# A three-part network on one core: one expert's slot search moves in line, its transposes later, and second products may run ahead

## The chip, the cores and the metric

The kernel runs on one core of a Trainium2 chip. The metric is the device time of one execution in microseconds (us); lower is better. Five engines work side by side, each through its own queue in order: PE (matrix products, transposes), DVE and ACT (elementwise work), POOL (here mostly a queue that starts DMAs with computed addresses or with addition) and SP (starts plain DMAs). "PEld" in the profile is the loading of a matmul's stationary operand.

## The reference, cut to what matters

```python
x = attention(r, k, v, w, u)               # 3072 tokens x 384, linear attention with decay
h = x @ w_in                               # dense part, 2048 hidden
x = (h * sigmoid(1.702 * h)) @ w_out
logits = x @ w_gate                        # 3072 x 8 experts
order = argsort(-logits.flatten())         # all (token, expert) pairs, best first
for idx in order:                          # greedy, each token once, each expert cap = 384 tokens
    tok, e = idx // E, idx % E
    if assigned[tok] >= 0 or counts[e] >= cap: continue
    assigned[tok] = e; counts[e] += 1
for e in range(8):                         # experts: 384 -> 1024 -> 384
    mask = assigned == e
    out[mask] = relu(x[mask] @ w1[e]) @ w2[e]
```

## The kernel before, in words

The first 580 us are the attention and the dense part, which the change does not touch. What follows is the part with the eight experts. They are handled in the order in which they fill up, and are called expert 0 to expert 7 here after that order. Two strands of work run side by side.

The first strand is the routing (`Router.route`, L304). For each expert in turn it

- searches (`search`, L382) for the threshold at which the next expert is full. A search has five rounds, each a comparison on DVE (L279), 24 small matmuls (L424), a small matmul (L429) and a maximum on DVE (L431), and each round needs the one before;
- writes the number of the expert found (`ei`, L323). From then on its weights can be loaded;
- ranks the tokens taken (L344 to L351), while the first steps for the next search (`best`, L236) are interleaved;
- marks the tokens that are left (`left`, L365) and goes on to the next search (its first instruction is L415).

Ranks must be turned into a list of 384 token numbers, `idx`. That is `slots` (L455): comparisons with 128 numbers on DVE (two of L476), 24 small matmuls (L487) and three small DVE steps, the last of which (L496) writes `idx`. For the first three experts (i <= 2, L358) `slots` runs in line, that is before the route goes on to `left` and the next search. For later ones `gather` (L1463) calls it, as a chain of its own that shares the engines with the next search.

`gather` then starts three indirect DMAs on POOL (L1476), which fetch 128 token rows each from `x2d` in device memory into the tile `cvb`. For each of the three, `land` (L1487) lets PE make three transposes (L1492), ACT a rounded copy (`xh`, L1501) and DVE the remainder (`xl`, L1503). When all three are through, the expert's products can begin (`o["ffn"]`, L1542).

The weights of an expert come as eight plain loads of 384 KB (L1415, SP). ACT makes the rounded half (L1434), and the remainder comes either from ACT (L1451) and a DMA with addition started on POOL (L1457), or from one DVE instruction (L1442). POOL also starts the scatter of the results (L1535).

The second strand is the loop of products (L1582), which consists of 64 steps, 8 to an expert. Step s issues a first product G1(s) (nine matmuls, L1086, reading `xh`, `xl` and the first weights) and then the second product G2(s-2) (nine matmuls, L1114). ACT and DVE turn the result of G1 into the input of G2 between them.

The order of all queues is written out while the program is built. A planner (`Issue`, L66) keeps a planned clock and planned busy times for each engine and for the DMA engines ("D"); each chain of work is a generator that yields until its planned time has come. `sc.until(cond)` (L117) advances the planned clock until the condition holds, issues whatever chain is due, and meanwhile issues small filler matmuls (`spin`, L687, line L690 in the profile). PE executes its queue in the order so written. If the planned time at which a transpose was placed is earlier than the real landing of its rows, PE stands still at that place, and all behind it with it.

The planned landing of gather a is `xt[a]`, the planned DMA time plus 1.4 (L1479). `land` waits for it, and for `LATE` = 4.0 more if the loop of products is still more than three steps ahead of the expert (`at[0] < NF3 * i - 3`, L1488). The loop waits for expert i at its first step (L1586), and only then issues G1 and the second product of two steps before.

Of the kernel before, what the change touches and what calls it, by code (L numbers as in the profile page):

```python
# [162 lines left out]
class Router:  # L163
# [140 lines left out]
    def route(self, out, i, found, taken):  # L304


        nc, NJ, E, L, t = self.nc, self.NJ, self.E, self.L, self.t
# [47 lines left out]
            n = next(fill, "end")  # L355
            yield from self.vec(0.22 if n == "end" else 0.47)
        out["rs"] = rs
        if i <= 2:  # L358
            yield from self.slots(out)
        taken()  # L360
        if i == E - 1:
# [139 lines left out]
def kernel(ctx, tc, r, k, v, w, rk, u, us, w_in, w_out, w_gate, w1, w2, out):  # L501
    nc = tc.nc
    V, A, P, T = nc.vector, nc.scalar, nc.gpsimd, nc.tensor
    H, D = u.shape
# [5 lines left out]
    E, NC3 = w1.shape[:2]  # L510
# [7 lines left out]
    NF3 = FE // 128  # L518
# [21 lines left out]
    DLAG = 1.5  # L540
    NPE = 8
    NHOLD = 12
    LATE = 4.0
    BEHIND = 1.0
    LASTF = 3

# [12 lines left out]
    sc = Issue()  # L559
# [5 lines left out]
    def wait(*names):  # L565
        while not all(R[n].ok() for n in names):
            yield 0.1
# [126 lines left out]
    Whi, Wlo, Wring, wdone = {}, {}, {}, set()  # L694
# [638 lines left out]
    ffn = {}  # L1333
    for s in range(len(seq) + 2):
# [4 lines left out]
        if s < len(seq):  # L1339
            blk, f = seq[s]  # L1340
# [9 lines left out]
        b2, f2 = seq[s - 2]  # L1350
# [37 lines left out]
    EX = [dict() for _ in range(E)]  # L1388
# [74 lines left out]
    def gather(i):  # L1463
# [5 lines left out]
        xg, xr, xt = [], [], []  # L1469
        for a in range(NU):  # L1470
            if a % 2 == 0:
                yield from wait("cvb")
                xr.append(R["cvb"].new())
                pair_ = cv.tile([128, 2, Dm], F32, name="cvb", bufs=NCVB)
            xg.append(pair_[:, a % 2])
            P.indirect_dma_start(out=xg[a], out_offset=None, in_=x2d,  # L1476
                                 in_offset=bass.IndirectOffsetOnAxis(ap=o["idx"][:, a:a + 1], axis=0))
            sc.busy["D"] = max(sc.busy["D"], sc.after((("P", 1.04),))) + 0.6
            xt.append(sc.busy["D"] + 1.4)  # L1479
        o["sent"] = True  # L1480
        sd = "xb" if i % 2 else "xa"
        yield from wait(sd)
# [4 lines left out]
        def land(a):  # L1487
            while sc.t < xt[a] + (LATE if at[0] < NF3 * i - 3 else 0.0):  # L1488
                yield 0.1
            ps, done = yield from bank()  # L1490
            for kt in range(KT):
                T.transpose(ps[:, kt * C:(kt + 1) * C], xg[a][:, kt * 128:(kt + 1) * 128], ident)  # L1492
            read.add(a)
            if read >= {0, 1}:
                R["cvb"].free(xr[0])
            if 2 in read:
                R["cvb"].free(xr[1])
            sl = slice(a * C, (a + 1) * C)
            px = ps[:, :NB].rearrange("p (k t) -> p k t", k=KT)
            yield (("T", 0.32),)  # L1500
            A.activation(xh[:, :, sl], px, AF.Copy)  # L1501
            yield (("A", 0.4),)
            V.tensor_tensor(xl[:, :, sl], px, xh[:, :, sl].bitcast(F32), op=OP.subtract)  # L1503
            done()
            yield (("V", 0.5),)
            left.discard(a)
# [37 lines left out]
    def routing():  # L1544
        for i in range(E):
            while at[0] < NF3 * (i - 2):
                yield 0.1

            def found():
                sc.add(weights(i), 1)  # L1550
                for ch in range(NC3):
                    for nm in ("raw1", "raw2"):
                        sc.add(split_weights(i, ch, nm), 2)

            def taken():
                sc.add(gather(i), 1)

            yield from router.route(EX[i], i, found, taken)
# [20 lines left out]
    sc.until(lambda: "ffn" in EX[0] and ("raw1", 0, 0) in wdone)  # L1579
    sc.spin = spin  # L1580
    R["g1"].free(wide_i)
    for s in range(E * NF3 + 2):  # L1582
        at[0] = s
        i, f = divmod(s, NF3)
        if i < E:
            sc.until(lambda: "ffn" in EX[i] and ("raw1", i, f // 2) in wdone)  # L1586
            EX[i]["ffn"].g1(f)
        if s >= 2:
            i2, f2 = divmod(s - 2, NF3)
            sc.until(lambda: ("raw2", i2, f2 // 2) in wdone)  # L1590
            if i2 < E - 1 or f2 < NF3 - LASTF:
                EX[i2]["ffn"].g2(f2)
    ffn = EX[E - 1]["ffn"]
    for f in range(NF3 - LASTF, NF3):
        ffn.begin(f)
# [61 lines left out]
```

## Time and profile before

| what | us |
|---|---|
| median of three runs | 865.42 |
| the three runs | 862.74, 865.42, 870.8 |
| the profiled execution's own time | 862.24 |
| its span, first to last instruction | 860.5 |

The profile belongs to the execution of 862.24 us, 1.7 us of which lie around the span. All times in the rows are counted from the start of the span.

### The profile page before, as it was taken

Reading aid. Unit: us, or ns where it says so; the run is one execution under the profiler, and the core shown is the slowest. Engines: PE = TensorE matmul, PEld = TensorE weight load, DVE = VectorE, ACT = ScalarE, POOL = GpSimd, SP = SyncE. Lnnn points to the kernel's source line nnn. Section 1 sums busy time; section 2 is a strip of 40 time slices with the busy share of each in tenths; the row PEclk is TensorE's granted clock in tenths of the full one; section 3 lists DMA queues with packets and bytes.
Section 4 is the critical chain, followed back from the end, with each engine's and each line's share of the span. In section 5 each row is a group of like instructions: output and inputs, shape, how many; then the busy total and the mean of one; then the engine's idle time right before and its main releaser. Section 6 shows DMA issues by size and latency. Waiting matters only on the chain.

```text
span 860.5 us, 17700 instructions
## 1 busy us (share of the span) xinstructions
PE 832.8 (97%) x6836; PEld 781.3 (91%) x6836; DVE 595.2 (69%) x1584; ACT 356.0 (41%) x687; POOL 140.1 (16%) x197
## 2 busy tenths in 40 slices
PE   7999999999999999999999999999999999999996
PEld 6788899999999999999999999987898988999995
DVE  8577678868876775866858747477886887875310
ACT  2254564343233334333333334305556555655521
POOL 3101000010100100000000100003334334434211
PEclk9899999999999999999999999999999999999998
DMA  9624442352321321322322100018889788989400
GB/s 262 181 85 127 144 138 85 115 165 74 97 76 53 107 80 58 89 79 79 92 55 81 35 3 28 1 56 219 205 232 255 217 200 228 278 216 322 103 28 27
DMA packets 46211, 107.04 MB, mean 124 GB/s; under 512 B 7368, under 2 KB 13360, under 8 KB 46128
## 3 DMA queue, kind: packets, MB, share of 16 engines
q1 hardware_dynamic: 30960, 69.26, 25.3%
q0 software_dynamic: 10416, 29.50, 15.9%
q10 hardware_dynamic: 4752, 7.17, 2.3%
q8 instruction: 53, 0.87, 0.4%
q14 instruction: 30, 0.25, 0.1%
HBM read 74.78 MB, written 10.03 MB: 99 GB/s over the span
## 4 chain that ended last, share of the span: by engine, by line
PE 80%; DMA 7%; issue 7%; DVE 3%; POOL 1%; ACT 1%; SPq 0%; POOLq 0%; ACTq 0%; DVEq 0%
PE g L1086 30%; PE acc L1114 29%; DMA cvb<-x2d,idx 5%; PE s L908 3%; PE s L1002 3%; PE s L424 2%; PE s L997 1%; PE acc L690 1%; PE s L752 1%; DMA raw<-in_w_out 1%; PE s L1239 1%; PE s L944 1%; PE s L1250 1%; DVE cvb L1163 1%; PE s L927 1%
## 5 line engine op out<-in xcount | busy, mean ns | idle before, releaser
L1114 PE MATMUL acc<-wk,gh 128*128 128x384 f32 x1080 | 282.3, 340 | 0.0
L1114 PEld LDWEIGHTS acc<-wk,gh 128*128 128x128 f32 x1080 | 193.1, 188 | 1.2 <-issue 0.5
L1114 PE MATMUL acc<-wk,gl 128*128 128x384 f32 x540 | 182.1, 337 | 0.0
L1086 PE MATMUL g<-xhb,wk 128*128 128x384 f32 x576 | 168.4, 342 | 1.4 <-DVE hold L1138 1.4
L1086 PE MATMUL g<-xha,wk 128*128 128x384 f32 x576 | 167.3, 340 | 0.0
L1132 ACT ACTIVATE g<-g 128x384 f32<-128x384 f32 x128 | 60.8, 475 | 215.0 <-PE g L1086 212.7
L1138 DVE TENSOR_TENSOR gl<-g,gh 128x384 fp32r<-128x384 f32 x116 | 64.2, 554 | 67.6 <-ACT gh L1135 66.8
L1086 PEld LDWEIGHTS g<-xhb,wk 128*128 128x128 f32 x576 | 106.2, 189 | 2.1 <-DVE hold L1138 1.7
L1086 PEld LDWEIGHTS g<-xha,wk 128*128 128x128 f32 x576 | 105.5, 188 | 0.7 <-issue 0.2
L1114 PEld LDWEIGHTS acc<-wk,gl 128*128 128x128 f32 x540 | 101.5, 188 | 0.0
L892 POOL TENSOR_SCALAR_AFFINE_SELECT At<-dg 128x512 f32<-128x512 f32 x42 | 31.2, 764 | 414.4 <-DVE dg L885 381.8
L1086 PE MATMUL g<-xlb,wk 128*128 128x384 f32 x288 | 97.5, 339 | 0.0
L1086 PE MATMUL g<-xla,wk 128*128 128x384 f32 x288 | 97.1, 337 | 0.0
L1163 DVE SCALAR_TENSOR_TENSOR cvb<-cva,raw 128x384 f32<-128x384 f32 x144 | 79.4, 552 | 10.8 <-ACT cva L1202 8.6
L1145 ACT ACTIVATE gh<-g 128x384 fp32r<-128x384 f32 x64 | 31.4, 491 | 95.3 <-PE g L1086 91.5
L1457 POOL DMA_DIRECT2D wk<-hold x51 | 46.6, 983 | 145.4 <-ACT wk L1451 82.4
L1148 DVE SCALAR_TENSOR_TENSOR gl<-g,gh 128x384 fp32r<-128x384 f32 x64 | 35.4, 553 | 47.7 <-ACT gh L1145 47.3
L1135 ACT ACTIVATE gh<-g 128x384 fp32r<-128x384 f32 x116 | 57.1, 492 | 7.1 <-ACT cva L1202 2.4
L1434 ACT ACTIVATE wk<-hold 128x768 fp32r<-128x768 f32 x64 | 53.3, 837 | 5.6 <-DMA hold<-in_w 4.9
L1086 PEld LDWEIGHTS g<-xlb,wk 128*128 128x128 f32 x288 | 54.4, 189 | 0.2
L1086 PEld LDWEIGHTS g<-xla,wk 128*128 128x128 f32 x288 | 54.2, 188 | 0.1
L915 DVE COPY_PREDICATED At<-later,s 128x512 f32<-128x512 uint8 x42 | 28.4, 727 | 33.5 <-PE s L908 33.5
(235 smaller groups left out, 1204.3 us busy)
## 6 DMA issues: line engine op xcount, KB each, us to landing
hold<-in_w SPq DMA_DIRECT2D x64, 384.0 KB, 7.1
wk<-hold POOLq DMA_DIRECT2D x51, 384.0 KB, 6.5
nat_m<-in_rk SPq DMA_DIRECT2D x18, 384.0 KB, 3.1
raw<-in_w_in SPq DMA_DIRECT2D x8, 768.0 KB, 4.9
raw<-in_w_out SPq DMA_DIRECT2D x8, 768.0 KB, 4.3
nat_v<-in_v SPq DMA_DIRECT2D x22, 256.0 KB, 2.9
nat_w<-in_w SPq DMA_DIRECT2D x22, 226.2 KB, 2.9
nat_k<-in_k SPq DMA_DIRECT2D x22, 224.0 KB, 2.7
```

The costliest lines, as they stand in the source:

```text
L892: P.affine_select(At[s], dg[:, s::2][:, :, None].to_broadcast([128, HP, C]), pattern=[[0, HP], [1, C]], compare_op=OP.is_equal, fill=0.0, ...
L915: V.copy_predicated(At[s], later[:, None, :].to_broadcast([128, HP, C]), pA[s][0].rearrange("p (a t) -> p a t", a=HP))
L1086: T.matmul(p, self.l1(kt, f, a), (self.xh, self.xl)[b_][:, kt], start=(kt == 0 and n == 0), stop=(kt == KT - 1 and n == 2))
L1114: T.matmul(self.acc[tt], gs[a][:, tt * C:(tt + 1) * C], self.r2(f, b_), start=(f in self.cuts and n == 0), stop=(end and n == 2))
L1132: A.activation(p, p, AF.Gelu_apprx_sigmoid)
L1135: A.activation(gh, p, AF.Copy)
L1138: V.tensor_tensor(gl, p, gh.bitcast(F32), op=OP.subtract)
L1145: A.activation(gh, p, AF.Relu)
L1148: V.scalar_tensor_tensor(gl, p, 0.0, gh.bitcast(F32), op0=OP.max, op1=OP.subtract)
L1163: V.scalar_tensor_tensor(scr[0][:, 0], x2, 1.0, wgB[e // 4][:, (e % 4) * Dm:(e % 4 + 1) * Dm], op0=OP.mult, op1=OP.mult, accum_out=router. ...
L1434: A.activation(Whi[key], raw, AF.Copy)
L1457: P.dma_start(out=Wlo[key].bitcast(F32), in_=raw, accum_op=OP.add)
```

## The change

The condition for `slots` in line becomes i <= 3, so the fourth expert (expert 3) has its list made before its route goes on. The planned landing of every gather but expert 0's is put 2.0 later (`LAND` = 3.4 in place of 1.4), and `LATE` falls from 4.0 to 2.0, so that the sum of both stays 5.4 where both apply. In the loop of products, a counter `second` tells how many second products have been issued. While a step's first product cannot be issued yet in the plan, second products of earlier steps are issued, one at a time, up to that of step s-1, before the loop waits.

```diff
-        if i <= 2:
+        if i <= 3:
             yield from self.slots(out)
...
-    LATE = 4.0
+    LATE = 2.0
+    LAND = 3.4
...
-            xt.append(sc.busy["D"] + 1.4)
+            xt.append(sc.busy["D"] + (LAND if i else 1.4))
...
+    second = [0]
+
+    def second_products(end):
+        while second[0] < end:
+            i2, f2 = divmod(second[0], NF3)
+            sc.until(lambda: ("raw2", i2, f2 // 2) in wdone)
+            if i2 < E - 1 or f2 < NF3 - LASTF:
+                EX[i2]["ffn"].g2(f2)
+            second[0] += 1
+
     for s in range(E * NF3 + 2):
         at[0] = s
         i, f = divmod(s, NF3)
         if i < E:
-            sc.until(lambda: "ffn" in EX[i] and ("raw1", i, f // 2) in wdone)
+            here = lambda: "ffn" in EX[i] and ("raw1", i, f // 2) in wdone
+            while not here() and second[0] < s:
+                second_products(second[0] + 1)
+            sc.until(here)
             EX[i]["ffn"].g1(f)
-        if s >= 2:
-            i2, f2 = divmod(s - 2, NF3)
-            sc.until(lambda: ("raw2", i2, f2 // 2) in wdone)
-            if i2 < E - 1 or f2 < NF3 - LASTF:
-                EX[i2]["ffn"].g2(f2)
+        second_products(max(0, s - 1))
```

## Rows read from the trace of the kernel before

**Rows 1.** The page's 40 slices of the span: TensorE clock and DMA share.
```profile
PEclk9899999999999999999999999999999999999998
DMA  9624442352321321322322100018889788989400
```
**Rows 2.** Stretches between experts' first products: stretch, length, busy per engine, clock, DMA share.
```profile
627.40:662.50 35.10, 33.49 (x306) 30.48 (x305) 26.69 (x105) 21.14 (x34) 15.34 (x19) 0.95 0.96 242
662.50:701.30 38.80, 37.00 (x393) 34.18 (x393) 30.94 (x123) 20.19 (x32) 13.66 (x18) 0.96 0.79 199
701.30:735.50 34.20, 32.21 (x310) 29.63 (x308) 28.82 (x118) 19.04 (x31) 14.75 (x18) 1.00 0.86 220
```
**Rows 3.** PE in order of time, at expert 3's start; in brackets idle before and releaser.
```profile
693.95 0.51 PE L690 MATMUL acc<-ident 128*128 128x128 bf16 x6
695.56 0.52 PE L1492 MATMUL s<-ident,cvb 128*128 128x128 f32 x3 [1.10 <-DMA cvb<-x2d,idx]
...
701.32 0.42 PE L1086 MATMUL g<-xhb,wk 128*128 128x384 f32 x1
...
703.13 0.51 PE L1114 MATMUL acc<-wk,gh 128*128 128x384 f32 x2
```
**Rows 4.** PE in order of time, the other transposes with idle time before them.
```profile
620.01 0.41 PE L1492 MATMUL s<-ident,cvb 128*128 128x128 f32 x2 [0.90 <-DMA cvb<-x2d,idx]
...
655.18 0.55 PE L1492 MATMUL s<-ident,cvb 128*128 128x128 f32 x3 [1.61 <-DMA cvb<-x2d,idx]
...
725.26 0.52 PE L1492 MATMUL s<-ident,cvb 128*128 128x128 f32 x3 [1.10 <-DMA cvb<-x2d,idx]
...
728.19 0.55 PE L1492 MATMUL s<-ident,cvb 128*128 128x128 f32 x3 [0.89 <-DVE sw L434]
...
758.62 0.55 PE L1492 MATMUL s<-ident,cvb 128*128 128x128 f32 x3 [0.53 <-DVE sw L434]
...
780.95 0.52 PE L1492 MATMUL s<-ident,cvb 128*128 128x128 f32 x3 [1.01 <-DMA cvb<-x2d,idx]
```
**Rows 5.** Two short stretches of the trace, columns as in rows 2.
```profile
656.70:660.10 3.40, 3.40 (x35) 2.98 (x33) 2.72 (x8) 2.73 (x5) 1.08 (x2) 0.50 1.09 209
...
697.70:701.10 3.40, 3.11 (x27) 3.08 (x28) 2.17 (x10) 2.31 (x5) 0.89 (x1) 0.50 0.50 93
```
**Rows 6.** DVE in order of time: the route of experts 2, 3 and 4.
```profile
638.48 0.15 DVE L323 TENSOR_SCALAR ei<-se 128x1 int32<-128x1 f32 x1
...
646.93 0.16 DVE L496 TENSOR_TENSOR idx<-r_tt 128x3 int32<-128x3 f32 x1
...
649.30 0.14 DVE L415 TENSOR_SCALAR q<-r_zero 128x1 f32<-128x1 f32 x1
...
671.86 0.14 DVE L323 TENSOR_SCALAR ei<-se 128x1 int32<-128x1 f32 x1
...
678.85 0.15 DVE L415 TENSOR_SCALAR q<-r_zero 128x1 f32<-128x1 f32 x1
...
689.22 0.16 DVE L496 TENSOR_TENSOR idx<-r_tt 128x3 int32<-128x3 f32 x1
...
701.26 0.15 DVE L323 TENSOR_SCALAR ei<-se 128x1 int32<-128x1 f32 x1
...
718.23 0.16 DVE L496 TENSOR_TENSOR idx<-r_tt 128x3 int32<-128x3 f32 x1
...
728.96 1.48 DVE L1503 TENSOR_TENSOR xla<-s,xha 128x384 fp32r<-128x384 f32 x3
```
**Rows 7.** The chain that ended last, in order of time: start, length, what.
```profile
647.88 7.25 DMA cvb<-x2d,idx
...
719.19 5.93 DMA cvb<-x2d,idx
...
783.21 1.56 PE acc L1114 x9
```
**Rows 8.** The gathers' line L1476 between 600 and 790 us: time to landing.
```profile
DMA to landing us min/median/max: 3.1/5.4/12.6
```

## The prediction, made before the changed kernel was run

> **What bounds the kernel now.** I read the 40 slices first, then the stretches by expert, then PE in order of time wherever it stood still, and last DVE's route and the chain of waits. The slices show that in the last 30% the DMA engines are 70 to 90% busy or more, which they are nowhere in the middle of the run, and that the TensorE clock is high throughout but for a slice at either end; a dent shorter than a slice doesn't show there [rows 1]. By expert, PE is busy almost throughout: 33.49 of 35.10, 37.00 of 38.80, 32.21 of 34.20 us [rows 2]. But these busy numbers hold filler matmuls and matmuls at half clock, so they hide the loss. Eight steps of two products need 16 times 1.56 us [rows 7], or 25.0, and the stretches are 34 to 39 long. Searches, transposes and slots explain some six of the rest, and waiting explains what is left. So I count what PE loses, wait by wait, and ask of each what the change does to it. What is not lost is work that stays.
>
> *Expert 3.* The last product of expert 2 that PE can do ends at 693.95, where fillers begin, and the first of expert 3 starts at 701.32 [rows 3]: 7.4 us. In these PE makes nine transposes (three times 0.52 [rows 3]) and one search round, for which I allow 0.6. The loss is 7.4 - 2.2 = 5.2. The cause is seen on DVE: the expert is known at 671.86, but `idx` comes only at 689.22 [rows 6], 17.4 us later, since `slots` shares DVE and PE with the next search. For expert 2, whose slots run in line, it is 638.48 to 646.93, 8.45 us.
>
> *Expert 2.* PE stands 1.61 us before its first transpose with products of expert 1 queued behind it [rows 4], and right after that the clock is granted at 0.50, the lower of its two levels (1.2 of 2.4 GHz), for 3.4 us [rows 5], in which half the speed costs 1.7. Together 3.3. The second dent, at 697.70, lies within expert 3's wait and is in its 5.2.
>
> *The others.* 0.90 (expert 1), 1.10 and 0.89 (expert 4), 0.53 (expert 5) and 1.01 (expert 6) [rows 4].
>
> The sum is 5.2 + 3.3 + 0.9 + 2.0 + 0.5 + 1.0 = 12.9 us. More than that the change cannot give, for it removes no work.
>
> **Part one, transposes later.** For experts 1 to 5 the loop is close when the rows come, so that the planned landing moves from 1.4 to 3.4. The rows show how wrong 1.4 was: 7.25 us from the first gather's issue to its landing at expert 2, and 5.93 at expert 4 [rows 7]. Two planned us more put one further first or second product (1.56 each) ahead of the transposes. At expert 2 that covers the 1.61, and with it the cause of the dent: of the 3.3 I leave 0.3 (between 0 and 3.3). At expert 1, 0.9 goes to 0 (0 to 0.9). It adds no instruction. Its cost is that `xh` and `xl` come up to 2 us later; that is hidden as long as PE still has products of the expert before, and costs up to 2 us at an expert for which PE is already waiting. Expert 6's transposes are planned far ahead, with 5.4 before and after, and I leave its 1.0 (0 to 2).
>
> **Part two, slots in line for expert 3.** Its twelve DVE instructions, 24 small matmuls and the three gathers behind them are moved, none added. With expert 2's losses shorter, the search for expert 3, in the middle of which they lie, ends earlier; I take 2.0 of 3.3 (0 to 3.3). So `ei` comes at 669.9 and `idx` 8.45 later, at 678.3, instead of 689.2. On POOL the three gathers now pass ahead of weight additions which they followed; on DMA they meet the loads of expert 3's weights, as expert 2's do. So I take that expert's 0.95 to the first issue and 7.25 to landing [rows 6, 7]: 686.5, and with two issues behind it and the conversions some 690.8 for the whole of `xl`. PE has work of expert 2 until 693.95 - 0.9 - 3.0 = 690.0; two search rounds move out of it (-1.4) and three transposes in (+1.5), 690.1. The cover of 0.7 us too little is made good by part three. Of the 5.2 I leave 0 (0 to 3).
>
> The price is paid by the next search. It started at 678.85 and now starts 2.37 after `idx`, as the one after expert 2 does (646.93 to 649.30 [rows 6]): 680.7, or 1.85 later. It took 22.4 us (to 701.26), with slots and PE's stop inside it; the one before took 22.6 with expert 2's stop inside. Without either I take 1.1 off (0 to 2.5). Expert 4 is then known at 702.0 instead of 701.26: 0.7 later, and later by up to 3.9 if nothing is won back (1.85 + 2.0), earlier by 1.5 if all goes well.
>
> **Part three, second products first.** Two second products, 3.1 us, can now fill a wait at the start of an expert. At expert 3 they were queued behind the first product (703.13 [rows 3]); they now reach 690.1 + 3.1 = 693.2, 2.4 us past the 690.8. It adds no instruction, and ACT and DVE have each of these second products' inputs ready one step before. If the cover were gone the two would cost nothing extra, only stay behind.
>
> **What is late next.** Expert 4, whose slots are still not in line. Its `xl` was complete at 730.4 (the end of 728.96 + 1.48 [rows 6]); with the route 0.7 later it is at 731.1. Expert 4's first product started at 735.5 [rows 2], with two second products open. PE now gets there earlier by all it no longer loses: 735.5 + 3.1 - (0.9 + 3.0 + 5.2 + 2.0) = 727.5, with the second products done. It waits 731.1 - 727.5 = 3.6 us. (The two stops before expert 4's transposes, 2.0, are absorbed in this wait.) Both dents of the clock now come out of a wait for a gather; this wait is filled with fillers, but transposes can again stand at the head. I add 0.8, between 0 and 1.7. For expert 5 PE comes 7 us earlier, and the slack there is larger (its loss now is 0.5), so I put 0.
>
> The page TensorE: Matmul & The Clock Gate of the Trainium skill, section HAM oscillation, holds that a matmul burst shorter than the DMA wait behind it makes the next one start cold. Here the dents follow waits for gathers [rows 3 to 5], which agrees, though one came after a single stop of 1.61 us. By that rule the wait that moves to expert 4 would cost the whole 1.7 in place of my 0.8, and the sum below would be 0.9 less.
>
> **The sum.** Left are 0.3 + 3.6 + 0.8 + 1.0 = 5.7 of 12.9: a gain of 7.2 us. Against the profiled execution that is 862.24 - 7.2 = 855.0. That execution is the fastest of the four times known; their middle is (862.74 + 865.42)/2 = 864.1, and the median of the runs alone 865.42. I forecast 864.1 - 7.2 = 856.9, 0.8% less. A measurement of this kernel can tell about 1%, 8.6 us, from no change.
>
> **Rivals.**
>
> *A. Expert 4 is not late.* If the search for it and its slots run 3 to 4 us faster without PE's stop, the wait of 3.6 and the 0.8 go too: gain 11.6, or 852.5. For it: 17 us from `ei` to `idx` (701.26 to 718.23) is twice what in-line slots need, so there is room. Against it: expert 4's own slots still compete with a search, and did so without any stop of PE. Chance 0.22.
>
> *B. The wait only moves.* The route gets nothing back, expert 4 is known 3.9 later, and its wait is 6.8 with 1.7 for the clock: gain 12.9 - 9.8 = 3.1, or 861. For it: searches with and without such stops have taken 22.4 and 22.6. Chance 0.22. Here belongs too that the change does not do what it says, since the planner may place expert 3's transposes late although its rows are there.
>
> *C. Slower: gathers drown in the weight traffic.* The DMA engines stand at 0.96, 0.79 and 0.86 [rows 2]. The 0.79 is the stretch that now gets 8 us shorter: 0.79 times 38.8 is 30.7 us of traffic in some 31 us, so it would be full. The longest landing of a gather is 12.6 [rows 8], 6.7 over expert 4's 5.93. If expert 4's landing takes that, on top of the 3.9 and of the 2.0 by which transposes are planned later, its `xl` comes 12.6 later, at 743.0. That is 15.5 after PE's 727.5, plus 1.7 for the clock and the 1.3 left elsewhere: 18.5 lost where 12.9 were lost, 5.6 us slower, 870. It decides from 8.4 us of delay on. Against it: expert 2's gathers had the fullest stretch and took 7.25. Chance 0.08. The page DMA: Bandwidth & Descriptors of the Trainium skill, section Issuing engines are not separate DMA queues, says that DMAs started from any engine run on the same 16 engines and interleave. By it the earlier gathers of expert 3 could gain no way round the loads of weights on SP; the rows fit it (7.25 in the 0.96 stretch, 5.93 in the 0.86 one).
>
> **How the numbers follow.** My forecast has 0.48, A 0.22, B 0.22, C 0.08. The forecast's own ends are gains of 4.5 and 9.5 us (the route between 3 later and 1.5 earlier, the clock between 0 and 1.7). The range reaches to A and 1.5 us further, for the spread of the runs, and on the other side past B into C: 851 to 866. Faster by over 1%: A and the upper third of the forecast, 0.22 + 0.16 = 0.38. Slower by over 1%: half of C, and 0.05 taken from the forecast for what I have not thought of in experts so full of DMA, 0.09. Within 1%: what is left of the forecast (0.27), B and half of C, 0.53.
>
> **What would show it.** `idx` of expert 3 before 681 and the first product of expert 3 at 690 to 694 show part two. No idle time over 0.5 before expert 2's transposes and no dent of the clock near 657 show part one. Two second products of expert 2 ahead of expert 3's first product show part three. A new wait with fillers ahead of expert 4's first product, which starts at 730 to 732, shows what is late next. The forecast is wrong if expert 4's `idx` does not stand within 717 to 722, or if a wait for weights, which no row shows now, appears in PE.

## The result, and the profile after

The changed kernel takes 869.82 us in the median of 20 runs (863.88 to 875.03), the kernel before 865.40 in 20 runs (859.21 to 870.80) on the same chip: a ratio of 1.0051 with a 95% interval of 1.0026 to 1.0075. The forecast was 856.9, with 851 to 866 for its range. The sign was wrong.

The profiled execution of the changed kernel took 869.79 us. Its line numbers are one higher than before's from the new constant on. The page's first line and two of its 40-slice rows, which answer to [rows 1]:

```profile
span 868.1 us, 17644 instructions
PEclk9899999999999999999999999998999999998998
DMA  9624442351322222212212000028896968989400
```

The DMA share of the last 30% is as high as it was, up to the last three slices, which the forecast's reading of [rows 1] passed over (4, 0 and 0 in both kernels). New are two 8s among the clock's nines, one for the slice of 586 to 608 us and one for that of 781 to 803 (a slice is 21.7 us).

One thing must be taken off before the two traces are laid side by side. The first expert product starts at 595.85 before and at 599.16 in the changed kernel, though the order of the instructions up to there is the same. Over all profiles of this study it starts anywhere between 595.6 and 603.6, in no order that follows the edits. So from here on I count from the first expert product where I compare kernels. From it to the end of the last second product it is 852.20 - 595.85 = 256.35 us before and 859.83 - 599.16 = 260.67 after: 4.3 us more, close to the difference of the medians (4.4). So the loss lies between these two marks. The two of the changed kernel, and below them those of before:

```profile
599.16 0.33 PE L1087 MATMUL g<-xha,wk 128*128 128x384 f32 x1
...
859.49 0.34 PE L1115 MATMUL acc<-wk,gl 128*128 128x384 f32 x1
```
```profile
595.85 0.34 PE L1086 MATMUL g<-xha,wk 128*128 128x384 f32 x1
...
851.86 0.34 PE L1114 MATMUL acc<-wk,gl 128*128 128x384 f32 x1
```

By stretch, with the columns of [rows 2]; the first four run from an expert's first product to the next expert's (experts 1, 2, 3 and 5), and the fifth is a short stretch inside expert 5. The sixth is expert 5's stretch in the kernel before:

```profile
629.20:666.10 36.90, 35.23 (x317) 32.26 (x315) 28.40 (x102) 20.26 (x32) 14.22 (x19) 0.95 0.91 239
666.10:700.60 34.50, 33.62 (x315) 31.25 (x315) 29.10 (x108) 19.46 (x32) 13.26 (x17) 1.00 0.84 218
700.60:738.80 38.20, 36.85 (x386) 33.62 (x385) 30.44 (x119) 20.40 (x33) 15.61 (x20) 0.96 0.71 183
771.20:805.40 34.20, 29.47 (x202) 28.05 (x202) 18.57 (x49) 17.75 (x30) 13.96 (x15) 0.90 0.89 281
790.10:796.90 6.80, 4.92 (x18) 4.35 (x19) 1.67 (x3) 1.47 (x3) 2.42 (x3) 0.50 1.06 307
...
769.00:798.10 29.10, 28.09 (x189) 27.37 (x188) 17.98 (x40) 18.74 (x33) 13.02 (x16) 1.00 0.99 292
```

The stretch before expert 3 did become shorter (34.5 where [rows 2] has 38.8), and the one after it became as much longer (38.2 where it was 34.2). And a loss has come up where the forecast had none: in expert 5's stretch the clock is granted at 0.90 on the mean, and for 6.8 us at 0.50, the lower of its two levels. That stretch takes 34.2 us where it took 29.1 before. Up to its start the changed kernel is 1.1 us ahead, counted from the first expert product, so nearly all of the 4.3 us is lost inside it. PE in order of time shows why (start, length, instructions; in brackets the idle time before and who ended it); these rows answer to [rows 3, 4]:

```profile
654.65 0.19 PE L424 MATMUL s<-oh,cvc 128*128 128x8 bf16 x2 [1.65 <-DVE oh L379]
...
700.57 0.33 PE L1087 MATMUL g<-xhb,wk 128*128 128x384 f32 x1
...
706.05 0.44 PE L1087 MATMUL g<-xhb,wk 128*128 128x384 f32 x1 [1.35 <-DVE gl L1149]
...
737.54 1.11 PE L691 MATMUL acc<-ident 128*128 128x128 bf16 x17
738.84 0.42 PE L1087 MATMUL g<-xha,wk 128*128 128x384 f32 x1
...
786.91 0.34 PE L1087 MATMUL g<-xhb,wk 128*128 128x384 f32 x1
791.98 2.48 PE L1493 MATMUL s<-ident,cvb 128*128 128x128 f32 x9 [4.73 <-DMA cvb<-x2d,idx]
```

Read them from the top. The stop before expert 2's transposes (1.61 in [rows 4]) is gone, but PE loses 1.65 us before a search's matmul at the same place. Expert 3 starts without a stop. Some 5 us later its third first product waits 1.35 for a remainder on DVE. Expert 4 starts at 738.84 behind fillers. And up to 791.98 PE stands 4.73 us before expert 6's transposes, which were queued after one matmul of a first product, the other eight of which follow them: real work stood behind the stop. PE is busy in 4.92 of the 6.8 us at half speed, which costs 2.5; with the stop that is 7.2 us, where [rows 4] has 1.01. The chain of waits passes through the same place (start, length, what), with a landing of 9.72 where [rows 7] has 7.25 and 5.93:

```profile
775.99 6.22 DMA out<-cva,idx
782.22 9.72 DMA cvb<-x2d,idx
...
791.98 2.48 PE s L1493 x9
```

### The profile page after: what moved, and what is told of

It reads as the page before. It is cut to its first block, busy times and chain, and to the rows that moved or that the text cites. A ratio compares the mean times of both kernels' runs of the same rounds, so it can differ in the third digit from the quotient of the medians.

```text
span 868.1 us, 17644 instructions
## 1 busy us (share of the span) xinstructions
PE 837.1 (96%) x6816; PEld 783.8 (90%) x6816; DVE 596.5 (69%) x1586; ACT 353.3 (41%) x685; POOL 138.7 (16%) x195
## 4 chain that ended last, share of the span: by engine, by line
PE 77%; issue 8%; DMA 7%; DVE 4%; POOL 2%; ACT 2%; SPq 0%; POOLq 0%; ACTq 0%; DVEq 0%
PE acc L1115 29%; PE g L1087 29%; PE s L909 3%; PE s L1003 3%; DMA hold<-in_w 2%; PE s L424 2%; DMA cvb<-x2d,idx 2%; PE s L998 1%; PE s L753 1%; DMA raw<-in_w_out 1%; PE s L1240 1%; PE s L945 1%; PE acc L691 1%; PE s L1251 1%; DVE cvb L1164 1%
## 5 line engine op out<-in xcount | busy, mean ns | idle before, releaser
L1115 PE MATMUL acc<-wk,gh 128*128 128x384 f32 x1080 | 282.4, 341 | 0.1
L1115 PEld LDWEIGHTS acc<-wk,gh 128*128 128x128 f32 x1080 | 193.7, 189 | 1.4 <-issue 0.8
L1115 PE MATMUL acc<-wk,gl 128*128 128x384 f32 x540 | 182.6, 338 | 0.0
L1115 PEld LDWEIGHTS acc<-wk,gl 128*128 128x128 f32 x540 | 101.8, 189 | 0.0
L1164 DVE SCALAR_TENSOR_TENSOR cvb<-cva,raw 128x384 f32<-128x384 f32 x144 | 79.3, 551 | 10.8 <-ACT cva L1203 8.6
```

The source lines that it names most:

```text
L1115: T.matmul(self.acc[tt], gs[a][:, tt * C:(tt + 1) * C], self.r2(f, b_), start=(f in self.cuts and n == 0), stop=(end and n == 2))
L1164: V.scalar_tensor_tensor(scr[0][:, 0], x2, 1.0, wgB[e // 4][:, (e % 4) * Dm:(e % 4 + 1) * Dm], op0=OP.mult, op1=OP.mult, accum_out=router. ...
```

## The experiments

The change has three parts, called here **slots** (expert 3's list in line), **landing** (transposes planned later) and **second** (second products ahead). The ratios below are to runs of the kernel before on the same chip, each with its 95% interval.

### Each part alone

```diff
-        if i <= 2:
+        if i <= 3:
```

> Only the slots of expert 3 in line; landing, LATE and the order of second products as before. T1 (the in-line slots push the route of the later experts back, so that expert 6's gathers meet the loads of two experts' weights): slower than before by 0.3 to 1.0%, with a stop of 3 us or more at expert 6's transposes. T2 (the loss comes from second products run ahead: three first products then follow each other with two banks to write to): faster by 0.3 to 0.8%, since expert 3 starts some 5 us earlier and nothing takes it back. T3 (the later transposes cost the time): faster by 0.3 to 0.8% as well.

Slots alone: 1.0029 (0.9996 to 1.0062). No gain, and a loss as T1 has it, but not clear of noise. The long stop that T1 names is not at expert 6: PE stood 2.19 us before expert 5's transposes (768), and the clock fell to half there.

```diff
-    LATE = 4.0
+    LATE = 2.0
+    LAND = 3.4
...
-            xt.append(sc.busy["D"] + 1.4)
+            xt.append(sc.busy["D"] + (LAND if i else 1.4))
```

> Only the planned landing: LAND 3.4 and LATE 2.0; slots and second products as before. T1 and T2: faster by 0.1 to 0.5%, as the stop of 1.6 us before expert 2's transposes and the clock's dent behind it go, with the wait at expert 3 (5.2 us) still there. T3 (the later transposes cost the time): slower by 0.3% or more, with xl of experts 4 to 6 complete some 2 us later.

Landing alone: 0.9913 (0.9881 to 0.9944). In its trace expert 2's transposes come without a stop, and the clock never falls to half in the expert phase. This is the part that works as forecast.

```diff
+            while not here() and second[0] < s:
+                second_products(second[0] + 1)
+            sc.until(here)
...
+        second_products(max(0, s - 1))
```

> Only the second products run ahead; slots and landing as before. T1 and T3: between the same and 0.3% faster, for two second products (3.1 us) fill the wait at expert 3. T2: slower by 0.3% or more, with an idle time of 1 us or more before the third first product behind each filled wait.

Second alone (`LAND` stays at 1.4): 0.9914 (0.9894 to 0.9935). It too gains 0.9% by itself, more than any of the three had it gain; T2, a loss, is out.

### The parts in pairs

```diff
+        if i <= 3:
+    LATE = 2.0
+    LAND = 3.4
```

> Slots in line and later landing, without the second products run ahead. T1: as the whole change, 0.2 to 0.8% slower than before, with the stop at expert 6. T2: faster by 0.4 to 1.0%. T3: slower by 0.3% or more, with the loss spread over the experts and none of it at one stop.

Slots and landing: 0.9988 (0.9963 to 1.0014). This trace and that of landing alone agree to 0.1 us up to expert 2, so what slots do can be read off this pair directly. The list came 8.5 us earlier (678.4 for 686.9), but the rows needed about 10 us to land, and PE and the search behind it stood before the transposes; the clock fell to half. First PE's stop, then a short stretch behind it with the columns of [rows 2] (clock 0.50), and then DVE's row at which expert 4 is known:

```profile
689.78 0.33 PE L1493 MATMUL s<-ident,cvb 128*128 128x128 f32 x1 [1.78 <-DMA cvb<-x2d,idx]
```
```profile
691.60:698.40 6.80, 6.04 (x40) 5.64 (x37) 4.61 (x14) 2.86 (x5) 0.47 (x1) 0.50 0.30 58
```
```profile
707.34 0.15 DVE L323 TENSOR_SCALAR ei<-se 128x1 int32<-128x1 f32 x1
```

With landing alone expert 4 is known at

```profile
698.76 0.15 DVE L323 TENSOR_SCALAR ei<-se 128x1 int32<-128x1 f32 x1
```

that is 8.6 us earlier. Of these, 4.5 are the later start of the search (680.8 for 676.3), and 4.0 its length (26.5 for 22.5). Expert 3 itself started 3.3 us later, not earlier (702.3 for 699.0), and the end came 7.2 us later (856.2 for 849.0). Buying expert 3's list was paid for with everybody's list after it.

```diff
+        if i <= 3:
+            while not here() and second[0] < s:
```

> Slots in line and second products run ahead, landing and LATE as before. T1: slower than before by 0 to 0.6%, like the slots alone, the 0.9% of the second products gone. T4: faster by 0.4 to 0.9%, the sum of 0.3% slower and 0.9% faster, as only the landing and the second products quarrel.

Slots and second: 0.9975 (0.9950 to 0.9999), between what T1 and T4 had.

```diff
+    LATE = 2.0
+    LAND = 3.4
+            while not here() and second[0] < s:
```

> Later landing and second products run ahead, slots in line only for the first three experts as before. T1 (the in-line slots spoil what the other two parts give): faster than before by 1.2 to 1.8%, about the sum of the two parts alone (0.9 and 0.9%). T4 (the two parts spoil each other, whatever the slots do): between 0.5% slower and 0.5% faster, as the whole change.

Landing and second: 0.9969 (0.9941 to 0.9996), as T4 has it, though each alone gives 0.991. Here expert 2 is known 43.95 us after the first expert product, against 41.45 with landing alone, and three stretches at half clock are back.

The eight kernels make a table (ratio to before, each to the runs of before on its own chip):

| | without second | with second |
|---|---|---|
| neither | 1 | 0.9914 |
| landing | 0.9913 | 0.9969 |
| slots | 1.0029 | 0.9975 |
| slots and landing | 0.9988 | 1.0051 |

Against the same kernel without them, slots cost between 0.3% and 0.8% in every company; the 0.3%, slots alone, is not clear of noise. Landing and second gain 0.9% each where they are alone, 0.3% together, and with slots the two together are slower than slots alone. The loss of the whole change is therefore no single part's.

### Attempts to mend expert 3

The next four take expert 3's late landing for the cause and shift its transposes, or let its gathers pass ahead of its weights.

```diff
-            xt.append(sc.busy["D"] + (LAND if i else 1.4))
+            xt.append(sc.busy["D"] + (LAND + (4.0 if i == 3 else 0.0) if i else 1.4))
```

> The whole change, with the planned landing of expert 3's gathers 4 us later still (7.4), so that its transposes stand further back in PE's queue. T1a (expert 3's early gathers land late, among the loads of its weights, PE stops at the transposes, the clock falls, and the search for expert 4 is held up with it): faster than the whole change by 0.4 to 1.0%, with no stop over 0.5 us before expert 3's transposes. T1b (the search for expert 4 merely begins later, by the time of the slots, and later experts follow it): the same as the whole change within 0.3%.

The whole change, expert 3's transposes 4 us later: 1.0071 (1.0049 to 1.0093), no better. Expert 3's transposes have no stop, but PE stands 1.57 us before expert 2's transposes (662), 1.76 in a search (708) and 4.47 before expert 6's transposes (798).

```diff
-                while i < 2 and ch == 1 and nm == "raw1" and "sent" not in o:
+                while (i < 2 or i == 3) and ch == 1 and nm == "raw1" and "sent" not in o:
...
-                if i < 2 and ch == 1 and nm == "raw1":
+                if (i < 2 or i == 3) and ch == 1 and nm == "raw1":
```

> The whole change, with expert 3's weights after the first two tiles loaded only behind its gathers, as experts 0 and 1 have it. T1a: gathers of expert 3 land within 5 us instead of some 8 to 10, and the kernel is faster than the whole change by 0.4 to 1.2%. T1b: the landing is shorter too, but the time is that of the whole change within 0.3%, or longer because the weights come later.

The whole change, with expert 3's weights from the third load on held back on SP until its gathers are issued: 1.0046 (1.0020 to 1.0072), no better.

```diff
+        if i <= 3:
+    LATE = 2.0
+    LAND = 3.4
+            xt.append(sc.busy["D"] + (LAND + (3.0 if i == 3 else 0.0) if i else 1.4))
```

> Slots in line and later landing without second products run ahead, and expert 3's planned landing 3 us later still (6.4). T5 (the in-line slots lose because expert 3's early transposes stand in PE's queue before their rows are there, and the clock falls and the search for expert 4 is held up behind them): no stop over 0.5 us before expert 3's transposes, the search for expert 4 within 23 us instead of 26.5, and a time of 0.988 to 0.994 of before, like the later landing alone. T6 (the slots lengthen the chain of searches by some 5 us, wherever the transposes stand, and the end follows the chain): the stop goes, but expert 4 is still known 4 us or more later than with the later landing alone (698.8 there), and the time is 0.996 to 1.003 of before.

Slots and landing, expert 3's transposes 3 us later: 1.0003 (0.9978 to 1.0028). The search for expert 4 shortened from 26.5 to 20.8 us, as it should if PE's stop had stretched it. But PE still stood 1.17 before expert 3's transposes, and the time did not fall. The landing of the three gathers of this kernel:

```profile
DMA to landing us min/median/max: 10.0/11.0/11.4
```

```diff
+        if i <= 3:
+    LATE = 2.0
+    LAND = 3.4
+                while (i < 2 or i == 3) and ch == 1 and nm == "raw1" and "sent" not in o:
```

> Slots in line and later landing, and expert 3's weights after the first two tiles loaded only behind its gathers. T5: the gathers land within 6 us instead of 10.4, expert 3's transposes don't stop PE, and the time is 0.988 to 0.994 of before. T6: the gathers land earlier, but expert 4 is known as late as without this, and the time is 0.996 to 1.003 of before.

Slots and landing, gathers ahead of the weights: 0.9924 (0.9900 to 0.9948), and the landing of the same three gathers:

```profile
DMA to landing us min/median/max: 3.8/4.7/5.6
```

The loads of 384 KB in flight made the difference between 11 us and 5. Expert 3 now starts 99.4 us after the first expert product (105.5 before). So the earlier list can be used without harm. But 0.9924 is no better than landing alone (0.9913): even then it brings nothing that the times show.

```diff
-        if i <= 2:
+        if i <= 1:
...
+    LATE = 2.0
+    LAND = 3.4
```

> Later landing, with one expert fewer in line: expert 2's slots too run beside the next search. T6: the chain of searches gets some 5 us shorter, experts 3 to 6 are known 3 to 6 us earlier, and the time is 0.2 to 0.8% below the later landing alone (0.983 to 0.990 of before), unless expert 2 itself is waited for. T5: nothing is gained by it, expert 2's rows come some 10 us later and PE waits for them: 0.3 to 1.0% above the later landing alone (0.994 to 1.002 of before).

One expert fewer in line, with landing: 0.9906 (0.9876 to 0.9936), the same as landing alone within the interval. Neither outcome that was set down separated itself: expert 4 is known 6.3 us earlier after the first expert product than with landing alone, and in exchange expert 2's first product comes 2.6 us later.

```diff
+    LATE = 2.0
+    LAND = 5.4
+            xt.append(sc.busy["D"] + (LAND if i else 1.4))
```

> Later landing alone, 2 us further: LAND 5.4 with LATE 2.0. If the gain of the later landing comes from PE no longer standing at transposes whose rows need 6 to 8 us to land, this takes another 0 to 0.3% off the later landing alone (0.988 to 0.992 of before); if 3.4 was already enough, xl comes 2 us later for nothing, and it is 0.992 to 0.997 of before.

Landing alone, two more us later: 0.9889 (0.9864 to 0.9914), the better of the two values set down, though not clear of landing at 3.4. No PE stop of over 1 us is left between 600 and 840.

### Three causes inside the whole change

What was still open was why slots with second and landing was slower than any pair. Three causes were tried, each as an edit of the whole change.

```diff
-            while not here() and second[0] < s:
+            while not here() and second[0] < s - 1:
```

> The whole change, but only one second product may run ahead (that of step s-2, which is due at the step anyway). O2 (both second products run ahead make three first products follow each other on two banks behind a filled wait, and PE stops there): 0.5% or more below the whole change, 0.995 to 1.001 of before, with no stop ahead of the third first product of expert 3. O1 and O3: as the whole change, 1.002 to 1.008.

Only one second product may run ahead, so that no three first products follow each other on two buffers (the 1.35 at 706.05): 1.0037 (1.0006 to 1.0067). The whole change has 1.0051, and the intervals overlap, so this is not the cause, or hardly. The edit doesn't isolate the 1.35, though: its trace has new stops of 1.62 and 2.01 us before the transposes of experts 2 and 5, and 2.38 before expert 6's.

```diff
-            while not here() and second[0] < s:
+            while f == 0 and not here() and second[0] < s:
```

> The whole change, but second products run ahead only at the first step of an expert, not where a later step waits for its weights (expert 0's third step in the trace). O1 (what is moved in expert 0 puts the searches of the first experts back): 0.5% or more below the whole change, 0.995 to 1.001 of before, with expert 2 known 2 us earlier after expert 0's first product. O2 and O3: as the whole change, 1.002 to 1.008.

Second products ahead only at an expert's first step: 0.9966 (0.9942 to 0.9990), 0.85% below the whole change. The condition of the change holds at every step. In expert 0 the planner has no weights for step 2 yet, so there it issued two second products ahead of the third first product. Expert 0 is the only expert in the changed kernel's trace where second products go ahead at a later step than the first (two at step 2, one at step 4). With the new condition the order there is before's. PE's rows in the changed kernel, and below them those with the new condition, in which the third first product comes before the first second product (L1115):

```profile
603.62 0.58 PE L1115 MATMUL acc<-wk,gh 128*128 128x384 f32 x2
...
607.96 0.33 PE L1087 MATMUL g<-xha,wk 128*128 128x384 f32 x1
```
```profile
603.34 0.42 PE L1087 MATMUL g<-xha,wk 128*128 128x384 f32 x1
...
605.12 0.51 PE L1115 MATMUL acc<-wk,gh 128*128 128x384 f32 x2
```

Behind it the route runs as forecast: from the list of expert 2 to the next search it took 649.67 - 647.29 = 2.38 us, where the forecast had 2.37. Its DVE rows, and below them those of the whole change, where it took 655.39 - 649.84 = 5.55:

```profile
647.29 0.16 DVE L496 TENSOR_TENSOR idx<-r_tt 128x3 int32<-128x3 f32 x1
647.37 0.17 DVE L366 TENSOR_SCALAR a<-rs 128x24 f32<-128x24 f32 x1
...
649.67 0.14 DVE L415 TENSOR_SCALAR q<-r_zero 128x1 f32<-128x1 f32 x1
```
```profile
649.84 0.16 DVE L496 TENSOR_TENSOR idx<-r_tt 128x3 int32<-128x3 f32 x1
651.97 0.56 DVE L1149 SCALAR_TENSOR_TENSOR gl<-g,gh 128x384 fp32r<-128x384 f32 x1 [1.97 <-ACT gh L1146]
652.45 0.17 DVE L366 TENSOR_SCALAR a<-rs 128x24 f32<-128x24 f32 x1
...
655.39 0.14 DVE L415 TENSOR_SCALAR q<-r_zero 128x1 f32<-128x1 f32 x1
```

In the whole change a remainder `gl` sits between the two steps of the route, and DVE stands 1.97 us before it for ACT. ACT in turn had stood before a weight conversion whose load had not landed:

```profile
650.72 0.85 ACT L1435 ACTIVATE wk<-hold 128x768 fp32r<-128x768 f32 x1 [2.17 <-DMA hold<-in_w]
651.47 0.47 ACT L1146 ACTIVATE gh<-g 128x384 fp32r<-128x384 f32 x1
```

Over the whole run ACT stands so for 10.0 us in the changed kernel and for 1.5 with the new condition (who waits, for whom: sum, times, longest), the changed kernel first:

```profile
ACT wk L1435 <- DMA hold<-in_w: 10.0, 7, 3.6
```
```profile
ACT wk L1435 <- DMA hold<-in_w: 1.5, 2, 0.9
```

The sum by itself doesn't tell the time: it is 4.9 us in the kernel before, and 12.2 with landing alone, which is faster than before. What the rows show is where one such wait stands, ahead of the route.

The expectation that expert 2 would be known two us earlier was missed: it came 41.5 us after the first product in both. The gain is made between its list and the next search, and behind.

```diff
-            xt.append(sc.busy["D"] + (LAND if i else 1.4))
+            xt.append(sc.busy["D"] + (LAND + (5.0 if i == 6 else 0.0) if i else 1.4))
```

> The whole change, with the planned landing of expert 6's gathers 5 us later (8.4). O3 (the whole change loses its time at expert 6, where transposes stop PE for 4.7 us with six products of expert 5 queued behind them, and the clock falls): that stop shrinks below 1 us, and the time is 0.4 to 0.9% below the whole change, 0.996 to 1.001 of before. O1 and O2: less than 0.3% below it, 1.002 or more.

The whole change, with expert 6's transposes planned 5 us later: 0.9968 (0.9940 to 0.9997), 0.83% below the whole change. The rows still need up to 10.2 us to land, but the stop before the transposes is 0.68 instead of 4.73, and expert 5's stretch is 27.6 us instead of 34.2.

Both edits together:

```diff
+            while f == 0 and not here() and second[0] < s:
...
+            xt.append(sc.busy["D"] + (LAND + (5.0 if i == 6 else 0.0) if i else 1.4))
```

> The whole change with both repairs: second products ahead only at the first step of an expert, and expert 6's planned landing 5 us later (8.4). If the two losses (O1 in expert 0, worth 0.85%, and O3 at expert 6, worth 0.83%) are separate and are all that spoils the whole change, their sum is due: 0.986 to 0.991 of before, with expert 3 starting 7 us or more earlier after expert 0's first product than before, and no stop over 1 us at expert 6. If they are one loss counted twice: 0.994 to 0.998.

0.9925 (0.9886 to 0.9963), 1.25% below the whole change. The two gains would add to 1.68%. The result lies between the two ranges set down, and its interval reaches into both, so whether the two losses overlap stays open. In its profile the way from the first to the last expert product is 844.89 - 595.73 = 249.16 us, 7.2 less than before. Its rows of DVE, and then of PE, are the ones in which the forecast's steps can be checked:

```profile
669.51 0.14 DVE L323 TENSOR_SCALAR ei<-se 128x1 int32<-128x1 f32 x1
678.30 0.17 DVE L496 TENSOR_TENSOR idx<-r_tt 128x3 int32<-128x3 f32 x1
681.99 0.14 DVE L415 TENSOR_SCALAR q<-r_zero 128x1 f32<-128x1 f32 x1
701.49 0.14 DVE L323 TENSOR_SCALAR ei<-se 128x1 int32<-128x1 f32 x1
729.63 0.55 DVE L1504 TENSOR_TENSOR xla<-s,xha 128x384 fp32r<-128x384 f32 x1
```
```profile
693.56 0.33 PE L1087 MATMUL g<-xhb,wk 128*128 128x384 f32 x1
...
730.26 0.23 PE L691 MATMUL acc<-ident 128*128 128x128 bf16 x1
730.30 0.42 PE L1087 MATMUL g<-xha,wk 128*128 128x384 f32 x1
...
784.05 0.33 PE L1493 MATMUL s<-ident,cvb 128*128 128x128 f32 x1 [1.28 <-DMA cvb<-x2d,idx]
```

### Versions that beat both kernels

```diff
+        if i <= 3:
+    LATE = 2.0
+    LAND = 5.4
+                while (i < 2 or i == 3) and ch == 1 and nm == "raw1" and "sent" not in o:
```

> No second products ahead; landing planned at 5.4, slots in line for expert 3, and its later weight loads behind its gathers. If the gains of the two kernels it is made of (0.9889 with 5.4 alone, 0.9924 with slots and gathers first) add up even in part, 0.982 to 0.989 of before; if the slots in line give nothing once PE no longer stands at transposes, 0.988 to 0.994.

No second products ahead, all transposes two us later still, expert 3's gathers ahead of its weights: 0.9893 (0.9860 to 0.9925). Again PE has no stop of over 1 us between 600 and 840, though expert 6's gathers took as long as 9.3 us there. With the one constant of 5.4 alone it was 0.9889, so the simplest version is as good as any: of the change, later transposes and nothing else. (In the one profile of each, the way from the first to the last expert product is 246.5 us here and 249.7 there; the times over all runs don't show that difference.)

```diff
-    LAND = 3.4
+    LAND = 5.4
...
+                while (i < 2 or i == 3) and ch == 1 and nm == "raw1" and "sent" not in o:
...
+            while f == 0 and not here() and second[0] < s:
```

> Landing planned at 5.4 for all, slots in line for expert 3, its later loads behind its gathers, and second products ahead at the first step of an expert only. If second products fill waits that are left at experts' starts (fillers before expert 4 in the same kernel without them), 0.2 to 0.5% below that kernel's 0.9893: 0.984 to 0.988. If the wait there is ended by the rows, not by products that are left, the same as without them: 0.987 to 0.992.

The same with second products ahead at an expert's first step: 0.9997 (0.9968 to 1.0027), 1% worse. The trap at expert 6 is open again; PE's row, and the stretch behind it:

```profile
782.00 0.90 PE L1493 MATMUL s<-ident,cvb 128*128 128x128 f32 x3 [2.64 <-DMA cvb<-x2d,idx]
```
```profile
781.90:785.30 3.40, 3.30 (x14) 3.15 (x15) 1.12 (x2) 1.12 (x3) 1.06 (x1) 0.55 1.06 296
```

A stop of 2.64 and 0.45 of 3.4 us for the clock (1.5) are 4.2, and the way from the first to the last product is 4.3 us longer than in the version without (250.8 for 246.5). The medians differ by 6.3 us and the ratios by 1.04%, or 9.0, so 2 to 5 us stay unexplained.

## Why the prediction was wrong, step by step

The forecast was a gain of 7.2 us, the measurement a loss of 4.4: 11.6 apart. The run with both edits wins back 1.25% of 865, or 10.8 us, of these. So two steps carry nearly all of the miss, and the others can be looked at in that run, in which the two are out of the way:

| step | forecast | with both edits |
|---|---|---|
| list of expert 3 | 678.3 | 678.30 |
| start of the next search | 680.7 | 681.99 |
| expert 3's first product | 690 to 694 | 693.56 |
| expert 4 known | 702.0 | 701.49 |
| end of expert 4's `xl` | 731.1 | 730.2 |
| expert 4's first product | 730 to 732 | 730.30 |
| gain, first to last product | 7.2 | 7.2 |

**Right**, then, are the times of part two's route and of expert 4's rows, to 1.3 us a step. The last row of the table is one profiled execution; over all its runs that kernel is 0.75% below before, where 0.8% was forecast.

**Right in part by luck** are the two rows on first products and the total. The forecast had PE out of work at 690.1 before expert 3 and covered until 693.2 by two second products. In this run no second product goes ahead of expert 3, and PE has work in the old order up to 693.56. The kernel before had the same products done at 693.95: PE is 0.4 us ahead there, not the 3.9 of "693.95 - 0.9 - 3.0". At expert 4 the forecast had PE ready at 727.5 and a wait of 3.6 with fillers; in the run PE gets there with one filler (730.26), so it came 2.7 us later and found the rows just complete. Earlier work that was put too early and waits that were put too long cancel.

**Wrong, part three.** The step that failed is "Two second products, 3.1 us, can now fill a wait at the start of an expert", with "If the cover were gone the two would cost nothing extra". The condition isn't about an expert's start; it holds at any step for which the plan lacks weights. It held in expert 0, and from there the order of ACT's and DVE's queues differs: by the list of expert 2 the next search starts 3.2 us later than it would have (5.55 for 2.38). Restoring the start-only meaning was worth 0.85%, about 7 us. That the condition at these steps of expert 0 is the cause is shown by the run that takes away all but an expert's first step. The plan behind it differs too, though: with the new condition no second product goes ahead of expert 3, where the changed kernel has two. By what way two second products in expert 0 leave ACT's weight conversions at the head of its queue before their loads land, 40 us later, was read from the rows, not tried. And it isn't a law: with second products alone the same reordering is there, and that kernel gained 0.9%.

**Wrong, part one at expert 6.** The step is "Expert 6's transposes are planned far ahead, with 5.4 before and after, and I leave its 1.0 (0 to 2)". The sum of 5.4 holds only while the loop is more than three steps ahead, that is, before step 45. Counted from the first expert product, the list of expert 6 came 6.1 us later than before (179.0 for 172.9). Its gathers were issued 8.4 later (183.1 for 174.7): another 2.3, because POOL was still in expert 4's scatters and two additions of weights. The loop came to step 45 at 187.8, 4.1 us earlier than before. So the transposes fell into step 45 in place of step 42, with a margin of 3.4 in place of 5.4. That the loop gets there early is enough: with second products ahead only at first steps, the list comes no later than before (172.9), the loop is at step 45 at 181.7, and PE stands 5.21 us. The rows also took longer to land than before's 4.5 to 7.6. POOL in order of time, and the landing of the three gathers behind it:

```profile
775.99 1.05 POOL L1536 DMA_INDIRECT out<-cva,idx  x1 [12.19 <-ACT cva L1534]
...
778.66 1.34 POOL L1536 DMA_INDIRECT out<-cva,idx  x1 [0.22 <-ACT wk L1452]
780.00 1.91 POOL L1458 DMA_DIRECT2D wk<-hold  x2
782.22 1.06 POOL L1477 DMA_INDIRECT cvb<-x2d,idx  x1 [0.30 <-issue]
```
```profile
DMA to landing us min/median/max: 8.6/9.1/9.7
```

That this costs the time is shown by the run that moves these transposes alone (0.83%). What it cost, 7.2 us in place of 1.0, would have taken most of the forecast's gain by itself.

**The rivals.** C had the right mechanism, a gather that takes 10 us amid weight loads, at the wrong expert: it put it at expert 4, and it struck at expert 6 here and at expert 3 with slots and landing alone. Its price for the whole kernel, 5.6 us, was close to the 4.4 measured by luck, since it was summed at expert 4; and I had given it a chance of 0.08. B, that the wait only moves, is nearest to what slots do: with landing, expert 4 is known 8.6 us later for them. A did not come.

**The checks named.** That PE does not stand before expert 2's transposes came true. No dent near 657 failed: the dent is there, from a search's stop and not from a transpose. Expert 3's list before 681 failed (685.08), and so did its first product at 690 to 694 (700.57), and expert 4's at 730 to 732 (738.84). Two second products did go ahead of expert 3's first product, and the new wait with fillers ahead of expert 4's is there (735.3 to 738.8). Expert 4's list, which had to stand within 717 to 722, came at 728.83 (at 718.65 with both edits). The wait for weights that would make the forecast wrong was not in PE. It was on ACT, where the forecast hadn't looked, and where the kernel before has one as well (4.9 us in all).

**What stays open**: why landing and second don't add (0.9969 where each has 0.991), the 2 to 5 us of the last version, and why an earlier list for expert 3, once harmless, brings nothing. For the first there is a candidate: in that pair too the two second products go ahead in expert 0, and from expert 2's list to the next search it takes 3.40 us, where each part alone has 2.37 or 2.38. The start-only condition was not tried there.

## What to carry to other kernels

When queues are written out ahead from a plan, ask of every wait not only how much slack it has, but at which step of the other strand it will now be placed: a stop with real work behind it can be paid twice, here with 4.73 us of idle time and 2.5 in the clock. A condition meant for one place must be read at every place where it is true. And parts that gain alone must be tried in pairs before they are called a sum: here two gains of 0.9% came to 0.3%, and the third part gained in none of its four pairings.

## What the runs showed of the hardware that was not expected

The first expert product starts between 595.6 and 603.6 us in profiles of kernels whose order up to there is the same, so a difference of up to 8 us between two profiles need not come from an edit. Three gathers of 128 rows each landed in 3.8 to 5.6 us when the weights' loads were held behind them, and in 10.0 to 11.4 when they were not. The clock fell to half after a search's stop of 1.65 us, and around the stop of 4.73 us it was at half for 6.8; after the 1.28 at expert 6 in the kernel with both edits it did not fall. But the length of the stop doesn't settle it: 6.8 us at half also followed a stop of 2.19 (slots alone, 768), and with landing at 5.4 the clock fell to half at 652.9 for 3.4 us, with no stop longer than 0.78 just before.
